# FNet block after squared-ReLU attention: three streams merged by time, channel DFT first, f32 loads of q and k

## The chip, the cores and the metric

One core of one Trainium2 chip. The metric is the device time of one launch in microseconds (us); before the change its median is 1024.95 us over three runs (1024.53 to 1026.13).

## The reference, cut to what matters

The batch B is 8, with 12 heads, 448 positions S and head size 64, so a row has D = 768 values; FFN's inner size is 3072. All inputs and the output are f32.

```python
scores = scale * np.matmul(q, k.transpose(0, 1, 3, 2))     # scale = 1/8
attn = np.maximum(scores, 0.0) ** 2 / S
x = np.matmul(attn, v)                                     # then heads side by side: (B, S, 768)
X = np.fft.fft(np.fft.fft(x, axis=1), axis=2)              # over positions, then over channels
u = x + np.real(X)
un = (u - mean) / np.sqrt(var + 1e-06)                     # over the 768 channels
out = u + np.maximum(un @ w_ch1, 0.0) @ w_ch2
```

## The kernel before, in words

All matmuls take bf16 operands. The kernel is written with a tile framework: the program gives instructions in an order, which is their priority; a scheduler with a model of the machine fixes each engine's queue from it at compile time, gives out the buffers of each tag, and sets the semaphores. On the chip every engine works through its queue in order. SP (which only starts DMAs), GpSimd (POOL) and the others have one queue each.

A batch has a front and an FFN part. The front (`front`, L361 on) is attention, then mixing. Attention (L171) takes two heads at a time (six such pairs, m). q and k come by casting DMAs on GpSimd's queue (L74), DVE copies them into another layout (L80), PE transposes them (L179, L180) into a PSUM tile, DVE copies them out as qT and kT (L187 to L189). For each of four blocks of key positions c, PE makes scores of two heads (L195), ACT applies ReLU (L198, rsc), DVE squares (L200, sq), and PE multiplies with v (L202), which adds up in av over the four blocks. DVE scales av into xT (L205). All the PSUM tiles of the front have one tag with three buffers of two banks (psA); FFN has two of one bank (psF).

Mixing (L210) transposes xT (L218), adds and subtracts positions s and S-s (xs, xa, L223, L224), takes the DFT over positions (L236), then over channels (L253) with half the outputs by symmetry, forms u for four row sets (DVE and GpSimd, L275, L276), its statistics and un (L304), and transposes un with an identity or a reversed one (L314) into unT. The rows of u go to a DRAM tile usc: the rows with natural order from u directly (112 rows, L284), the reversed ones after a shuffle on DVE into urev, in four blocks of 31 or 32, 32, 32 and 17 or 16 rows (L288, L292).

FFN works on groups of 384 or 512 rows (8 groups; a pair of batches gives one of each). The first matmul has 24 output blocks j of six matmuls each (L339), with ReLU on ACT (L342) into one hT tile per j. The second (L352) goes over 128-row chunks and two halves of 384 columns, 24 matmuls each; DVE adds the residual o (L354), which SP reloads from usc (L347), and SP stores the rows (L356). The tile o has the tag "o" with two buffers; urev has the same tag.

The program's order is front(0), front(1), then for each b: front(b+2), ffn(b). Weights are loaded once, by casting DMAs on GpSimd's queue (L92, L99), between the loads of the first two batches.

Of the kernel before, what the change touches and what calls it, by code (L numbers as in the profile page):

```python
# [9 lines left out]
FP32 = mybir.dt.float32  # L10
BF16 = mybir.dt.bfloat16
I32 = mybir.dt.int32
# [9 lines left out]

@with_exitstack
def kernel(
# [14 lines left out]
    R1 = R + 1  # L39
    MC = D // 128  # L40
    JC = FF // 128
    NQ = S + 2
    COL = [0, R1, 2 * R1, 2 * R1 + R]
    ROWS = [R1, R1, R, R]
    NS = S // 2 + 1
    KH = D // 4 + 1
    HG = 4
    NG = H // HG

# [12 lines left out]
    def psF():  # L62
        return psum.tile([128, 512], FP32, name="psF", tag="F", bufs=2)


    def load_qkv(b):
        tiles = []
        for g in range(NG):
            hs = slice(g * HG, (g + 1) * HG)
            row = []  # L70
            for nm, src in (("q", q), ("k", k), ("v", v)):
                t = work.tile([R, 2 * HG, 2 * Dh], BF16, name=f"{nm}n", tag=f"{nm}n",
                              bufs=4 if nm == "v" else 2)
                nc.gpsimd.dma_start(  # L74
                    out=t, in_=src[b, hs].rearrange("h (f p j) d -> p (h f) (j d)", f=2, j=2))
                t = t.rearrange("p (h f) (j d) -> p (f j) h d", f=2, j=2)
                if nm != "v":

                    o = work.tile([R, 4, HG, Dh], BF16, name=f"{nm}r", tag=f"{nm}r", bufs=2)
                    nc.vector.tensor_copy(o, t)  # L80
                    t = o.rearrange("p c h d -> p c (h d)")
                row.append(t)
            tiles.append(row)
        return tiles
# [19 lines left out]
    ident = const.tile([128, 128], BF16, name="ident")  # L104
    make_identity(nc, ident)
    ubot = []
    for i in range(2):
        t = const.tile([128, D], FP32, name=f"ubot{i}")
        nc.gpsimd.memset(t[96:128, :], 0.0)
        ubot.append(t)  # L110

    rev = const.tile([128, R1], BF16, name="rev")
    nc.gpsimd.memset(rev, 0.0)
    nc.gpsimd.affine_select(out=rev, in_=rev, compare_op=ALU.not_equal, fill=1.0, base=-R,
                            pattern=[[1, R1]], channel_multiplier=1)
    zero_t = const.tile([128, 1], FP32, name="zero_t")
    nc.gpsimd.memset(zero_t, 0.0)
    eps_t = const.tile([128, 1], FP32, name="eps_t")
    nc.gpsimd.memset(eps_t, 1e-6)
    qT_bufs = []  # L120
    for i in range(3):
        t = const.tile([128, R1 + 1 + 4 * R], BF16, name=f"qT{i}")
        nc.gpsimd.memset(t[:, R:R + 2], 0.0)
        qT_bufs.append(t)

    def sincos(dst, y, n, p):

        r = work.tile([128, 4 * KH], FP32, name="dftr", tag="o", bufs=2)
        nc.vector.tensor_scalar(r[:p, :n], y[:p, :n], float(2 ** 23), float(2 ** 23),
                                op0=ALU.add, op1=ALU.subtract)  # L130
        nc.vector.tensor_tensor(y[:p, :n], y[:p, :n], r[:p, :n], op=ALU.subtract)
        nc.scalar.activation(dst, y[:p, :n], AF.Sin, bias=zero_t[:p], scale=2.0 * math.pi)

    def build_dft():

        seq = const.tile([R1, 4, NS], BF16, name="seqm")
        col = work.tile([128, 2 * KH], FP32, name="dcol", tag="qs", bufs=1)
        row = const.tile([128, 8], FP32, name="drow")
        nc.gpsimd.iota(col[:, 0:NS], pattern=[[1, NS]], base=0, channel_multiplier=0,
                       allow_small_or_imprecise_dtypes=True)  # L140
        nc.gpsimd.iota(row[:, 0:2], pattern=[[1, 2]], base=0, channel_multiplier=2,
                       allow_small_or_imprecise_dtypes=True)
        nc.vector.tensor_scalar(row[:, 0:2], row[:, 0:2], 1.0 / S, None, op0=ALU.mult)
        for t in range(2):
            y = work.tile([128, 4 * KH], FP32, name="dfty", tag="u", bufs=2)
            for i in range(2):
                nc.vector.tensor_scalar(y[:R1, i * NS:(i + 1) * NS], col[:R1, 0:NS],
                                        row[:R1, i:i + 1], 0.25 if t == 0 else 0.0,
                                        op0=ALU.mult, op1=ALU.add)
            sincos(seq[:, 2 * t:2 * t + 2, :].rearrange("p a s -> p (a s)"), y, 2 * NS, R1)  # L150

        col2 = work.tile([128, 2 * KH], FP32, name="dcol2", tag=f"t{ALU.add}", bufs=1)
        nc.gpsimd.iota(col2, pattern=[[1, 2], [2, KH]], base=0, channel_multiplier=0,
                       allow_small_or_imprecise_dtypes=True)
        nc.gpsimd.iota(row[:, 4:7], pattern=[[128, 3]], base=0, channel_multiplier=1,
                       allow_small_or_imprecise_dtypes=True)
        nc.vector.tensor_scalar(row[:, 4:7], row[:, 4:7], 1.0 / D, None, op0=ALU.mult)
        chan = []
        for m in range(3):
            t = const.tile([128, 2, 2 * KH], BF16, name=f"chan{m}")  # L160
            y = work.tile([128, 4 * KH], FP32, name="dfty", tag="u", bufs=2)
            for i in range(2):
                nc.vector.tensor_scalar(y[:, i * 2 * KH:(i + 1) * 2 * KH], col2,
                                        row[:, 4 + m:5 + m], 0.25 if i == 0 else 0.0,
                                        op0=ALU.mult, op1=ALU.add)
            sincos(t.rearrange("p a s -> p (a s)"), y, 4 * KH, 128)
            chan.append(t)
        return seq, chan


    def attention(b, tiles):  # L171
        xT = []
        for m in range(MC):
            qn, kn, vn = tiles[m // (HG // 2)]
            h0 = (2 * m) % HG
            pt = psA(BF16)
            for c in range(4):
                hs = slice(h0 * Dh, (h0 + 2) * Dh)
                nc.tensor.transpose(pt[:, 0, c * R:(c + 1) * R], qn[:, c, hs], ident[:R, :R])  # L179
                nc.tensor.transpose(pt[:, 1, c * R:(c + 1) * R], kn[:, c, hs], ident[:R, :R])  # L180
            qT = qT_bufs[m % 3]
            kT = work.tile([128, S], BF16, name="kT", tag="kT", bufs=3)
            pq = pt[:, 0, 0:S].rearrange("p (c r) -> p c r", c=4)

            qa = qT[:, 0:4 * R1].rearrange("p (c r) -> p c r", c=2)[:, :, 0:R]
            qb = qT[:, R1 + 1:R1 + 1 + 4 * R].rearrange("p (c r) -> p c r", c=2)[:, :, 0:R]
            nc.vector.tensor_copy(qa, pq[:, 0:2, :])  # L187
            nc.vector.tensor_copy(qb, pq[:, 2:4, ::-1])
            nc.vector.tensor_copy(kT, pt[:, 1, 0:S])  # L189
            av = psA()  # L190
            for c in range(4):
                sc = psA()
                for e in range(2):
                    ps = slice(e * Dh, (e + 1) * Dh)
                    nc.tensor.matmul(sc[:R, e, 0:NQ], lhsT=kT[ps, c * R:(c + 1) * R], rhs=qT[ps, 0:NQ],  # L195
                                     start=True, stop=True)
                r = work.tile([R, 2, NQ], BF16, name="rsc", tag="rsc", bufs=2)
                nc.scalar.activation(r, sc[:R, :, 0:NQ], AF.Relu)  # L198
                s = work.tile([R, 2, NQ], BF16, name="sq", tag="sq", bufs=3)
                nc.vector.tensor_tensor(s, r, r, op=ALU.mult)  # L200
                for e in range(2):
                    nc.tensor.matmul(av[e * Dh:(e + 1) * Dh, 0, 0:NQ], lhsT=vn[:, c, h0 + e, :],  # L202
                                     rhs=s[:, e, :], start=(c == 0), stop=(c == 3))
            x = work.tile([128, NQ], BF16, name="xT", tag=f"xT{m}", bufs=1)
            nc.vector.tensor_scalar(x, av[:, 0, 0:NQ], 1.0 / (64.0 * S), None, op0=ALU.mult)  # L205
            xT.append(x)
        return xT


    def mix(b, xT, seq, chan, unT):  # L210
        xn, xs, xa = [], [], []
        for par in range(2):
            n = ROWS[2 * par]
            px = psA(BF16)
# [152 lines left out]
    def front(b):  # L367
        xT = attention(b, loaded.pop(b))
        if b + 2 < B:
            loaded[b + 2] = load_qkv(b + 2)  # L370
# [45 lines left out]
```

## Time and profile before

| | us |
|---|---|
| median of three runs | 1024.95 |
| lowest, highest | 1024.53, 1026.13 |
| the profiled execution | 1024.24 |
| its span, first to last instruction | 1022.4 |
| PE, DVE, ACT, GpSimd busy in the span | 766.5, 413.4, 324.8, 117.3 |
| mean granted clock of PE | 0.824 |

PE's granted clock has two levels, 1.2 GHz (0.5) and 2.4 GHz (1.0). PE's matmuls overlap in the records: the mean duration of one is longer than the distance from one start to the next, and the busy time counts overlaps once. A chain of waits is followed back from the last instruction to what released each one.

### The profile page before, as it was taken

Reading aid. Unit: us, or ns where it says so; the run is one execution under the profiler, and the core shown is the slowest. Engines: PE = TensorE matmul, PEld = TensorE weight load, DVE = VectorE, ACT = ScalarE, POOL = GpSimd, SP = SyncE. Lnnn points to the kernel's source line nnn. Section 1 sums busy time; section 2 is a strip of 40 time slices with the busy share of each in tenths; the row PEclk is TensorE's granted clock in tenths of the full one; section 3 lists DMA queues with packets and bytes.
Section 4 is the critical chain, followed back from the end, with each engine's and each line's share of the span. In section 5 each row is a group of like instructions: output and inputs, shape, how many; then the busy total and the mean of one; then the engine's idle time right before and its main releaser. Section 6 shows DMA issues by size and latency. Waiting matters only on the chain.

```text
span 1022.4 us, 11062 instructions
## 1 busy us (share of the span) xinstructions
PE 766.5 (75%) x4404; PEld 406.9 (40%) x4416; DVE 413.4 (40%) x862; ACT 324.8 (32%) x484; POOL 117.3 (11%) x139
## 2 busy tenths in 40 slices
PE   2653995566599563999499764799679865599998
PEld 1222443224254232545254323444444424366554
DVE  3477457445402546155700547235720345400001
ACT  2441761432124422065114431146104442122220
POOL 6411012011100102011200112000200000100000
PEclk9996998556599656999799756799979955699999
DMA  9993242242311332253220332332030000321202
GB/s 143 202 203 65 28 46 47 35 43 21 115 31 11 36 35 85 78 62 37 83 64 1 36 37 45 104 66 28 23 109 16 1 1 13 106 90 31 62 10 84
DMA packets 83716, 59.70 MB, mean 58 GB/s; under 512 B 68304, under 2 KB 71376, under 8 KB 83664
## 3 DMA queue, kind: packets, MB, share of 16 engines
q0 software_dynamic: 70528, 25.96, 21.4%
q1 hardware_dynamic: 13136, 33.04, 11.2%
q8 instruction: 34, 0.56, 0.2%
q14 instruction: 18, 0.15, 0.0%
HBM read 62.91 MB, written 22.02 MB: 83 GB/s over the span
## 4 chain that ended last, share of the span: by engine, by line
PE 65%; DVE 17%; ACT 9%; DMA 5%; issue 2%; POOL 0%; SPq 0%; ACTq 0%; DVEq 0%; POOLq 0%
PE psF L352 21%; PE psF L339 21%; PE psA L202 7%; ACT rsc L198 7%; PE psA L195 7%; DVE sq L200 3%; DMA usc<-urev 3%; PE psA L179 2%; PE psA L218 2%; DVE stats L280 2%; PE psA L236 2%; PE psA L253 2%; DMA o<-usc 1%; PE psA L180 1%; DVE u L276 1%
## 5 line engine op out<-in xcount | busy, mean ns | idle before, releaser
L352 PE MATMUL psF<-w,hT 128*128 128x384 bf16 x1344 | 239.5, 336 | 11.8 <-DVE o L354 11.8
L198 ACT ACTIVATE rsc<-psA 112x900 bf16<-112x900 f32 x192 | 168.9, 918 | 220.5 <-PE psA L195 220.5
L339 PE MATMUL psF<-unT,w 128*128 128x384 bf16 (+1 forms) x1140 | 237.1, 354 | 1.6 <-ACT hT L342 0.6
L200 DVE TENSOR_TENSOR sq<-rsc 112x900 bf16<-112x900 bf16 x192 | 120.3, 626 | 172.1 <-ACT rsc L198 172.1
L352 PEld LDWEIGHTS <-hT 128*128 128x128 bf16 x1344 | 133.4, 101 | 106.5 <-issue 29.7
L342 ACT ACTIVATE hT<-psF 128x384 bf16<-128x384 f32 (+1 forms) x192 | 104.0, 543 | 215.5 <-PE psF L339 214.4
L339 PEld LDWEIGHTS <-w 128*128 128x128 bf16 x1152 | 107.5, 98 | 114.6 <-issue 21.3
L202 PE MATMUL psA<-sq,vn 112*64 112x450 bf16 x384 | 93.5, 475 | 63.1 <-DVE sq L200 61.8
L354 DVE TENSOR_TENSOR o<-psF,o 128x384 f32<-128x384 f32 x56 | 30.6, 556 | 228.3 <-PE psF L352 212.4
L195 PE MATMUL psA<-qT,kT 64*112 64x450 bf16 x384 | 88.7, 494 | 37.2 <-DVE kT L189 18.0
L314 PE MATMUL psA<-ident,un 112*128 112x112 bf16 x96 | 18.7, 296 | 99.3 <-DVE un L304 99.3
L202 PEld LDWEIGHTS <-vn 112*64 112x64 bf16 x384 | 29.2, 118 | 118.4 <-issue 83.6
L195 PEld LDWEIGHTS <-kT 64*112 64x112 bf16 x384 | 32.6, 154 | 87.7 <-issue 54.3
L314 PEld LDWEIGHTS <-un 112*128 112x128 bf16 (+1 forms) x192 | 16.2, 137 | 109.3 <-DVE un L304 109.3
L187 DVE COPY qT<-psA 128x224 bf16<-128x224 bf16 x48 | 13.1, 273 | 114.1 <-PE psA L180 114.1
L74 POOL DMA_DIRECT2D qn<-in_q_dram x24 | 20.0, 835 | 315.8 <-DVE qr L80 239.5
L276 POOL TENSOR_TENSOR ubot<-tpm,xn 113x383 f32<-113x383 f32 (+1 forms) x16 | 13.5, 846 | 264.7 <-DVE tpm L262 237.3
L239 ACT ACTIVATE ytmp<-psA 128x450 f32<-128x450 f32 x24 | 13.1, 546 | 81.8 <-PE psA L236 60.8
L179 PE MATMUL psA<-ident,qr 112*128 112x112 bf16 x192 | 32.5, 254 | 8.4 <-DVE qr L80 8.0
L74 POOL DMA_DIRECT2D vn<-in_v_dram x24 | 19.7, 819 | 163.2 <-PE psA L202 161.4
L205 DVE TENSOR_SCALAR xT<-psA 128x450 bf16<-128x450 f32 x48 | 30.1, 627 | 16.0 <-PE psA L202 14.3
L180 PE MATMUL psA<-ident,kr 112*128 112x112 bf16 x192 | 32.8, 256 | 2.3 <-DVE kr L80 2.3
(68 smaller groups left out, 598.7 us busy)
## 6 DMA issues: line engine op xcount, KB each, us to landing
o<-usc SPq DMA_DIRECT2D x28, 384.0 KB
qn<-in_q_dram POOLq DMA_DIRECT2D x24, 224.0 KB, 4.2
kn<-in_k_dram POOLq DMA_DIRECT2D x24, 224.0 KB, 4.9
vn<-in_v_dram POOLq DMA_DIRECT2D x24, 224.0 KB, 4.1
usc<-u SPq DMA_DIRECT2D x16, 336.0 KB
w<-in_moe_w_ch_dram POOLq DMA_DIRECT2D x12, 384.0 KB, 11.9
w<-in_moe_w_ch_dram POOLq DMA_DIRECT2D x4, 1152.0 KB, 22.8
usc<-urev SPq DMA_DIRECT2D x40, 96.0 KB
```

The source lines that it names most:

```text
L74: nc.gpsimd.dma_start(out=t, in_=src[b, hs].rearrange("h (f p j) d -> p (h f) (j d)", f=2, j=2))
L179: nc.tensor.transpose(pt[:, 0, c * R:(c + 1) * R], qn[:, c, hs], ident[:R, :R])
L180: nc.tensor.transpose(pt[:, 1, c * R:(c + 1) * R], kn[:, c, hs], ident[:R, :R])
L195: nc.tensor.matmul(sc[:R, e, 0:NQ], lhsT=kT[ps, c * R:(c + 1) * R], rhs=qT[ps, 0:NQ], start=True, stop=True)
L198: nc.scalar.activation(r, sc[:R, :, 0:NQ], AF.Relu)
L200: nc.vector.tensor_tensor(s, r, r, op=ALU.mult)
L202: nc.tensor.matmul(av[e * Dh:(e + 1) * Dh, 0, 0:NQ], lhsT=vn[:, c, h0 + e, :], rhs=s[:, e, :], start=(c == 0), stop=(c == 3))
L314: nc.tensor.matmul(pu[:, e, i * R:(i + 1) * R], lhsT=uns[i][:n, ms], rhs=idn, start=True, stop=True)
L339: nc.tensor.matmul(ph[:, 0:N], lhsT=w1_sb[m][j // (JC // 2)][:, jj * 128:(jj + 1) * 128], rhs=unT[:, m, 0:N], start=(m == 0), stop=(m == M ...
L342: nc.scalar.activation(h[:, 0:N], ph[:, 0:N], AF.Relu)
L352: nc.tensor.matmul(pc[:, 0:D // 2], lhsT=hT[j][:, c * 128:(c + 1) * 128], rhs=w2_sb[j // 6][:, j % 6, hs], start=(j == 0), stop=(j == JC - 1))
L354: nc.vector.tensor_tensor(o[:, hs], pc[:, 0:D // 2], o[:, hs], op=ALU.add)
```

## The change

The order of the program becomes a merge of three kinds of streams by a clock of their own: each stream says, at each yield, how much time its last piece stands for, and the piece of the stream with the least time comes next. Attention of all batches is one stream, each batch's mixing one, FFN of all batches one. FFN of batch b is let in when mixing b has been written out. The scheduler is told to use its timeline model.

Inside attention, scores run two steps ahead of the products with v (LAG). q and k are loaded as f32 by SP, two groups of four heads ahead, and the re-layout copy casts them; v stays on GpSimd's queue, with three buffers. kT is copied by ACT. The order of positions in qT is natural and mirrored halves (225 columns each), so that sums and differences of s and S-s are taken on xT itself (fold), and of channels c and c+384 (A and Bm). Mixing takes the DFT over channels first, straight from these, 225 positions in two chunks of 113 and 112, then over positions with 385 output columns. There is no shuffle: the mirrored rows go to a second DRAM tile ubo as they are, and a DMA from DRAM to DRAM copies them reversed into usc. The reload of o is asked for in the middle of the first matmul, and o shares its buffers with no tile of mixing; the output needs one store per chunk. The PSUM tiles are psS (two of two banks), psT and psF (two of one bank each).

The diff, cut to its core:

```diff
-    def psA(dtype=FP32):
-        return psum.tile([128, 2, n], dtype, name="psA", tag="A", bufs=3)
+    def psS():
+        return psum.tile([128, 2, 512], FP32, name="psS", tag="S", bufs=2)
+    def psT(dtype=FP32):
+        return psum.tile([128, n], dtype, name="psT", tag="T", bufs=2)
...
+                if nm == "v":
+                    t = work.tile([R, 2 * HG, 2 * Dh], BF16, name="vn", tag="vn", bufs=3)
+                    nc.gpsimd.dma_start(out=t, in_=src)
+                else:
+                    t = work.tile([R, 2 * HG, 2 * Dh], FP32, name=f"{nm}n", tag=f"{nm}n", bufs=QB)
+                    nc.sync.dma_start(out=t, in_=src)
...
+    def heads(b, m):
+        if h0 == 0:
+            relay(g)
+            load_group("qk")
+        pt = psF(BF16) if b == 0 else psT(BF16)
...
+        nc.scalar.activation(kT, pt[:, S:2 * S], AF.Copy)
...
+        for i in range(4 * MC + LAG):
+            if i < 4 * MC:
+                if c == 1 and m + 1 < MC:
+                    hd[m + 1] = heads(b, m + 1)
+                if c == 3 and m % 2 == 0:
+                    load_group("v")
+                sc = scores(i)
...
+                    x = work.tile([128, NQ], BF16, name="xT", tag=f"xT{m}", bufs=1)
+                    nc.vector.tensor_scalar(x, av[:, 0:NQ], 1.0 / (64.0 * S), None, op0=ALU.mult)
+                    nc.vector.tensor_tensor(f[:, 0, :], x[:, 0:NS], x[:, NS:NQ], op=ALU.add)
+                    nc.vector.tensor_tensor(f[:, 1, :], x[:, 0:NS], x[:, NS:NQ], op=ALU.subtract)
...
+        for n0, n1 in SC:
+            pp = psS()
+            for t in range(2):
+                for kp, Y, kw in ((0, A, KH), (1, Bm, KH - 1)):
+                    for m in range(3):
+                        nc.tensor.matmul(pp[:n, t, kp * KH:kp * KH + kw], lhsT=Y[m][:, t, n0:n1],
+                                         rhs=chan[m][:, t, kp * KH:kp * KH + kw],
+                                         start=(m == 0), stop=(m == 2))
...
+            nc.sync.dma_start(out=usc[r0 + s0:r0 + s1, :], in_=us[0][:n])
+            lo, hi = (1, R1) if ch == 0 else (0, n - 1)
+            t0 = r0 + S - s0 - (hi - 1)
+            nc.sync.dma_start(out=ubo[t0:t0 + hi - lo, :], in_=us[1][lo:hi])
+            nc.sync.dma_start(
+                out=usc[t0:t0 + hi - lo, :].rearrange("t (a d) -> a t d", a=2)[:, ::-1, :],
+                in_=ubo[t0:t0 + hi - lo, :].rearrange("t (a d) -> a t d", a=2))
...
+        for j in range(JC):
+            if j in (JC // 2, JC // 2 + 2):
+                reload()
...
+                if m % 3 == 2:
+                    yield 3 * N / 2400
...
+    constants()
+    load_group("qk")
+    load_group("v")
+    load_group("qk")
+    load_group("v")
+    seq, chan = build_dft()
     load_w1(0)
     load_w1(1)
     load_w2()
...
+            n = 4 * MC + LAG + 1
+            rate = STEP0 if b == 0 else STEP1 if b == 1 else (73.0 / n)
+            for d in attention(b, *x):
+                yield d * rate
+            spawn(mix_stream(b, x))
...
+            while b not in mixed:
+                yield 1.0
+            for d in ffn(*groups[b]):
+                yield d * (STRETCH if b < B - 1 else 1.0)
...
+    STEP0, STEP1, STRETCH = 1.1, 2.4, 1.33
+    spawn(attention_stream())
+    while streams:
+        s = min(streams)
+        clock[0] = s[0]
+        d = next(s[2], None)
...
+    with tile.TileContext(tc.nc, schedule_with_timeline_sim=True) as t:
+        body(t, *args)
```

## Rows read from the trace of the kernel before

**Rows 1.** The page: busy us of each engine; two of its costliest groups.

```profile
PE 766.5 (75%) x4404; PEld 406.9 (40%) x4416; DVE 413.4 (40%) x862; ACT 324.8 (32%) x484; POOL 117.3 (11%) x139
...
L198 ACT ACTIVATE rsc<-psA 112x900 bf16<-112x900 f32 x192 | 168.9, 918 | 220.5 <-PE psA L195 220.5
...
L200 DVE TENSOR_TENSOR sq<-rsc 112x900 bf16<-112x900 bf16 x192 | 120.3, 626 | 172.1 <-ACT rsc L198 172.1
```

**Rows 2.** Busy time by stretch: us, length, engines' busy us, PEclk, DMA share, GB/s.

```profile
0.00:104.00 104.00, 47.22 (x246) 24.66 (x247) 57.99 (x124) 33.48 (x43) 35.03 (x60) 0.91 1.00 151
104.00:158.00 54.00, 52.80 (x344) 25.36 (x342) 28.38 (x59) 32.91 (x52) 7.36 (x9) 0.99 0.40 39
158.00:271.00 113.00, 57.02 (x327) 32.04 (x325) 65.33 (x139) 32.27 (x44) 18.95 (x17) 0.58 0.30 48
...
409.00:483.00 74.00, 73.37 (x463) 37.50 (x462) 30.15 (x61) 31.15 (x47) 7.36 (x9) 0.98 0.40 61
483.00:510.00 27.00, 13.43 (x106) 9.19 (x104) 18.69 (x41) 5.43 (x10) 5.79 (x4) 0.78 0.24 69
```

**Rows 3.** SP's longest wait from 104 to 271 us: total us, times, longest.

```profile
SPq L284 <- DVE u L276: 146.7, 4, 74.8
```

**Rows 4.** Timeline of SP's issues in the same stretch: start us, us, what.

```profile
264.77 1.71 SPq L292 DMA_DIRECT2D usc<-urev  x4
267.36 2.14 SPq L347 DMA_DIRECT2D o<-usc  x2
```

**Rows 5.** The chain of waits at the end: start us, us, what, pieces merged.

```profile
955.46 10.74 PE psF L339 x49
...
986.27 31.21 PE psF L352 x192
```

**Rows 6.** Timeline of PE near 119 us, clock 1.0: start us, us, what.

```profile
118.71 0.40 PE L195 MATMUL psA<-qT,kT 64*112 64x450 bf16 x2
119.04 0.34 PE L339 MATMUL psF<-unT,w 128*128 128x384 bf16 x1
119.38 0.38 PE L202 MATMUL psA<-sq,vn 112*64 112x450 bf16 x2
119.69 0.22 PE L179 MATMUL psA<-ident,qr 112*128 112x112 bf16 x1
...
120.09 0.33 PE L339 MATMUL psF<-unT,w 128*128 128x384 bf16 x1
```

**Rows 7.** The chain of waits from 483 to 512 us.

```profile
489.83 1.27 PE psA L253 x13
...
498.80 8.11 DMA usc<-urev
```

**Rows 8.** The page: GB/s in 40 slices of 25.6 us; issues of the weight loads.

```profile
GB/s 143 202 203 65 28 46 47 35 43 21 115 31 11 36 35 85 78 62 37 83 64 1 36 37 45 104 66 28 23 109 16 1 1 13 106 90 31 62 10 84
...
w<-in_moe_w_ch_dram POOLq DMA_DIRECT2D x12, 384.0 KB, 11.9
w<-in_moe_w_ch_dram POOLq DMA_DIRECT2D x4, 1152.0 KB, 22.8
```

**Rows 9.** Groups of PE's matmuls from 420 to 480 us: count | busy us, mean ns | idle before.

```profile
L339 PE MATMUL psF<-unT,w 128*128 128x384 bf16 x144 | 29.6, 328 | 0.1
L352 PE MATMUL psF<-w,hT 128*128 128x384 bf16 x93 | 15.4, 326 | 0.0
L202 PE MATMUL psA<-sq,vn 112*64 112x450 bf16 x46 | 8.8, 374 | 0.0
L195 PE MATMUL psA<-qT,kT 64*112 64x450 bf16 x43 | 7.5, 377 | 0.3
L179 PE MATMUL psA<-ident,qr 112*128 112x112 bf16 x20 | 2.6, 214 | 0.1
```

**Rows 10.** Busy time, clock, DMA share and GB/s around the stores of u.

```profile
255.50:257.50 2.00, 0.00 (x0) 0.00 (x0) 2.00 (x7) 0.00 (x0) 0.00 (x0) 0.53 0.55 167
261.20:262.40 1.20, 0.62 (x5) 0.23 (x3) 1.20 (x4) 0.00 (x0) 1.20 (x1) 0.50 0.11 20
```

More of the change, by code (lines that the diff above doesn't have):

```diff
@@ L23, with body @@
 @with_exitstack
-def kernel(
+def body(
     ctx: ExitStack,
@@ L56 @@
     usc = dram.tile([B * S, D], FP32, name="usc")
-    def psA(dtype=FP32):
+    ubo = dram.tile([B * S, D], FP32, name="ubo")
+    def psS():
+        return psum.tile([128, 2, 512], FP32, name="psS", tag="S", bufs=2)
+    def psT(dtype=FP32):
         n = 512 if dtype == FP32 else 1024
-        return psum.tile([128, 2, n], dtype, name="psA", tag="A", bufs=3)
[L62 to L84, printed above, removed]
@@ new lines, in body, with load_group @@
+    loads = [[None] * 3 for _ in range(B * NG)]
+    loaded = {"qk": 0, "v": 0}
+    def load_group(what):
+        i = loaded[what]
+        if i == B * NG:
+            return
+        loaded[what] += 1
+        b, g = divmod(i, NG)
+        hs = slice(g * HG, (g + 1) * HG)
+        for nm, src in (("q", q), ("k", k), ("v", v)):
+            if nm in what:
+                src = src[b, hs].rearrange("h (f p j) d -> p (h f) (j d)", f=2, j=2)
+                if nm == "v":
[4 more added lines that the diff above has]
+                    nc.sync.dma_start(out=t, in_=src)
+                loads[i]["qkv".index(nm)] = t
@@ L101, in load_w2 @@
             w2_sb[i] = t
[L104 to L168, printed above, removed]
@@ L171, in attention @@
[L171 to L196, printed above, removed]
@@ new lines, in attention, with scores @@
+    def attention(b, xT, A, Bm):
+        def scores(i):
+            m, c = divmod(i, 4)
+            qT, kT = hd[m][0:2]
+            sc = psS()
+            for e in range(2):
+                ps = slice(e * Dh, (e + 1) * Dh)
+                nc.tensor.matmul(sc[:R, e, 0:NQ], lhsT=kT[ps, c * R:(c + 1) * R], rhs=qT[ps, :],
+                                 start=True, stop=True)
+            return sc
+        hd = {0: heads(b, 0)}
+        yield 1.0
+        F, sc, sqs = [], {}, {}
+        for i in range(4 * MC + LAG):
+            if i < 4 * MC:
+                m, c = divmod(i, 4)
+                if c == 1 and m + 1 < MC:
[3 more added lines that the diff above has]
+                sc = scores(i)
@@ L204, in attention @@
[L204 to L214, printed above, removed]
+                sq = work.tile([R, 2, NQ], BF16, name="sq", tag="sq", bufs=3)
+                nc.vector.tensor_tensor(sq, r, r, op=ALU.mult)
@@ new lines, in mix @@
+                x = work.tile([R1, D], BF16, name="xn", tag=f"xn{i}", bufs=1)
+                nc.scalar.activation(x[:n], px[:n, 0:D], AF.Copy)
+                xs.append(x)
+                yield 0.7
+            pq = psS()
+            for t in range(2):
+                for i, (n0, n1) in enumerate(SC):
+                    nc.tensor.matmul(pq[:n, t, 0:KN], lhsT=seq[:n1 - n0, t, i, s0:s1],
+                                     rhs=pcs[i][:n1 - n0, t, 0:KN], start=(i == 0), stop=(i == 1))
+            qs = work.tile([R1, KN], FP32, name="qs", tag="qs", bufs=1)
@@ new lines, in mix @@
+            yield 2.5
+        if b % 2 == 0:
+            g0 = work.tile([128, MC, 512], BF16, name="unT", tag="unT", bufs=2)
+            tail = work.tile([128, MC, S - 384], BF16, name="tail", tag="tail", bufs=1)
+            groups.append((b * S, 384, g0))
+            tails.append(tail)
+            unT = [(g0, 0, 0, 384), (tail, 0, 384, S)]
+        else:
+            g1 = work.tile([128, MC, 512], BF16, name="unT", tag="unT", bufs=2)
+            groups.append(((b - 1) * S + 384, 512, g1))
+            nc.gpsimd.tensor_copy(g1[:, :, 0:S - 384], tails.pop())
+            unT = [(g1, S - 384, 0, S)]
```

303 lines of the change are left out of this document (182 added, 121 removed).

## The prediction

> **What bounds the kernel now.** I read the page first, then busy time by stretch, the waits and order of SP's queue, and the chain of waits. The page [rows 1] has TensorE (PE) busy for three quarters of the span and no other engine above 40%, so it names PE, but as a mean over two kinds of stage. The stretches [rows 2] part them. From 104 to 158 us and from 409 to 483 PE is busy for 98 and 99% of the time at a granted clock of 0.99 and 0.98 (2.4 GHz nearly throughout): attention runs there with FFN matmuls between its steps. From 158 to 271 PE is busy for 57 of 113 us at 0.58, so mostly at 1.2 GHz: attention and mixing run alone. From 483 to 510 mixing alone keeps PE busy for 13 of 27 us. The first 104 us have no FFN work by construction.
>
> Why is there no FFN work from 158 to 271, when group 0 was ready? SP's queue tells [rows 3, 4]: the reload of the residual (o<-usc, L347) is issued at 267.4, behind the four-piece stores of batch 2's u, and in that stretch SP waited 146.7 us for DVE to make u. The tile o shares its two buffers with the reversed copy urev of a later batch, so the reload stands behind work that comes much later. FFN's second matmul needs o to free its PSUM tile, its first needs hT, and the whole stream stands. So the bound is a starved PE, not PE's work.
>
> **PE's work, priced at 2.4 GHz.** An FFN matmul of 384 columns takes 31.21/192 = 0.1625 us, one of 512 columns 10.74/49 = 0.219 [rows 5]. There are 1344 + 576 of the first and 576 of the second: 312.0 + 126.2 = 438.2. By start-to-start times [rows 6] a pair of scores takes 119.04 - 118.71 = 0.33, a pair of AV products 0.31, and eight transposes 0.40; 192 of each pair and 48 sets of eight give 122.9 + 19.2. None of this changes.
>
> Mixing changes. Channel first, it has 192 matmuls of 193 columns at 1.27/13 = 0.098 [rows 7] = 18.8, 64 of 385 columns at 0.1625 = 10.4 (96 + 96 of 225 columns go), 192 transposes of 128 columns at 0.057 (0.05 scaled by 128/112) = 11, and 192 of 112 at 0.05 = 9.6: about 50. In all 630 us, 78.8 per batch, of which 24 per batch are attention and mixing.
>
> **Parts that stay beside PE.** DVE: copies of k, xn, the sums xs and xa, yp, ym and the shuffle go: 160 instructions of the size of a square's 0.626 us [rows 1], about 100 us. Folds and differences (144 of 225 or 450 elements, by the square's 900 elements 0.16 to 0.31 us each), half the DFT copy (16) and a re-layout that now reads f32 (48, each up to 0.5 us longer) come: between 40 and 90, I take 70. DVE goes from 413 [rows 1] to about 385 us. ACT gains 48 copies of k, 32 of xn and 16 of the channel result, 0.4 to 0.8 us each by the 0.918 for 900 elements [rows 1], and loses 24 ytmp: from 325 to about 370. Beside 640 us of PE, both are some 60% used: no bound, but denser than the 41 and 42% of the stretch 409 to 483 [rows 2]. Without that cover each of their microseconds would count, as it does in the opening. GpSimd loses 48 DMA issues; SP gains them. SP's q/k loads are asked for two head groups ahead, about 48 us, and can hide a wait of that length.
>
> **The opening, 97 us.** Before, FFN begins at about 104 [rows 2]. The first steps get shorter: scores run two steps ahead, so a step costs max(ACT 0.918 [rows 1], DVE 0.626 plus an estimated 0.75 for its share of copies and folds) = 1.4 us, 24 steps 34 us. But the third v load is emitted inside attention, behind all weight loads on GpSimd's one queue. Weights are 12 x 384 + 4 x 1152 KB = 9.44 MB; at 203 GB/s [rows 8] that is 46.5 us. Add two v loads (2.3), six f32 q/k loads of 0.46 MB on the same saturated engines (7 to 14, by 406 GB/s read or 203 written; I take 9), a start of 3 and a landing of 2 (both estimates): v arrives at 63, while its first use is due at 14 (an estimate: first loads, and the DFT tables on DVE) + 16 x 1.4 = 36. PE has nothing else then: three squared tiles and two score tiles fill up and attention stands. After 63 come the eight AV steps, five at full pace (9 us), then mixing alone, 27 us now [rows 2], 25 taken: FFN starts at 97.
>
> **The steady part, 653 us.** What is left is 630 - 24, less 6 of batch 1's attention done beside mixing: 600. The last group's 62 us are pure FFN at the prices above. The other 538 run interleaved. How well does that go? From 420 to 480 [rows 9]: 237 FFN matmuls x 0.1625 = 38.5, 23 pairs x 0.31, 21.5 x 0.33 and 40 transposes x 0.05 are 54.7 of 60 us, 0.91. It holds a step of attention per 2.8 us, the 73/27 = 2.7 of the new merge. So 538/0.91 = 591, + 62 = 653.
>
> **Hand-overs, 10.** FFN of batch b is emitted just as mixing b ends. Mixing's chain is 27 us now with nothing beside it, and the merge gives it 22 units. At about 3 us each for seven batches, half of it filled by attention: 10.
>
> **The residual by way of DRAM: 0 to 60, 5 taken.** The shuffle and four row blocks become a store of 113 or 112 rows to usc, one of 112 or 111 rows to ubo, and a copy from ubo to usc that SP issues only when ubo has landed; behind it in SP's queue stand q/k loads, reloads and output stores. No row shows a copy from DRAM to DRAM or a store of 113 rows. The nearest: the 112-row store moves its 0.34 MB in the two microseconds at 167 GB/s; in 261.2 to 262.4, the tail of the 31- and 17-row stores, a busy share of 0.11, under two of 16 engines, moves 20 GB/s [rows 10], and those 48 rows, 147 KB, hold the chain for 8.11 us [rows 7], 18 GB/s. So 113 rows cost 2 to 347 KB/20 = 17.4 us, a copy 2 to 17. The ends are far apart; of the row counts shown, 112 and 32 are fast and 31 and 17 slow, and 113 and 111 are odd like the slow ones, so I take 17 for both stores and 10 for a copy. In line on one engine the four transfers of a batch land 17 + 10 + 17 + 10 = 54 us after the first starts, some 12 before mixing ends: 42 after its end. The reload is first used some 40 us after mixing ends (24 blocks j and a half chunk, beside attention), and the chunk that needs copied rows 10 later: covered, narrowly; hence 5. As a load, the four take 38 to 68 us of that engine per batch, its sixteenth of some 7.6 MB of other traffic (q, k, v, reload, output) at 20 GB/s another 24: 62 to 92, against 78.8/0.91 = 87 of PE.
>
> The Trainium skill (DMA: Bandwidth & Descriptors, section "Why a DMA increments its semaphore by 16 and not by 1") says that a transfer is spread over the largest number up to 16 that divides the outermost extent of both sides. The 31- and 17-row rows agree; by it 113 rows go to one engine, 111 to three, and the copy, whose outermost extent is its two halves, to two: 17 + 6 + 2 x 9 to 17 = 41 to 57 us in place of 38 to 68, and the 5 stay. If transfers spread over all engines whatever their rows, the term is 0 and the sum 5 lower.
>
> **End and sum.** After the last matmul the reload's add and store took 1022.4 - (986.27 + 31.21) = 4.9. Span: 97 + 653 + 10 + 5 + 5 = 770. The profiled execution takes 1024.24 with a span of 1022.4, so 1.8 lie around it, and it stands 0.7 below the median of the runs, 1024.95. Forecast: 772.
>
> **Rivals.** *v is not late* (the scheduler or the rings let it pass): FFN starts at 14 + 34 + 25 = 73, total 748; with interleaving at 0.97 instead of 0.91 and no hand-over loss 702. For: 0.97 is still under the 73.4 of 74 us that PE is busy in [rows 2]. Against: one queue, and earlier loads come first in the program. Chance 0.18.
>
> *SP's wait shows*: the landing of ubo is late behind the 113-row store, and reloads, stores and q/k loads stand behind it in order, as they stand behind u now [rows 3, 4]. If 5 to 13 us of each batch come through: 810 to 870. For: the margin of 8 us above. Chance 0.17.
>
> *The merge holds only half*: each engine's order is fixed from a model; where the chip is later, PE waits in order. A pair of batches now takes 239 us (271 to 510), 119 each; the new one 87; halfway is 103: 97 + 7 x 103 + 62 = 880. If nothing held, the change would not do what it says, and the time would lie between 97 + 7 x 119 + 62 = 992 and today's. For: denser ACT and DVE. Against: the fed stretches come from such an order too. Chance 0.09, of it 0.01 for no change.
>
> *Slower*: one DMA engine becomes the bound. It must need over 87 + (1025 - 772)/7 = 123 us per batch, so each copy over (123 - 58)/2 = 32 us, twice the 17 of a slow store of as many bytes. At 35 us a copy the total is 772 + 7 x (128 - 87) = 1059. For: no row shows DRAM to DRAM. Against: no row shows so low a rate. Chance 0.04.
>
> **How the numbers follow.** The forecast keeps 0.52, with its own range 730 to 810 (interleaving 0.87 to 0.96, opening 90 to 105). To hold eight in ten, the range takes in the early v and most of SP's wait: 700 to 870. What can be told from no change is 0.2%, 2 us (the runs of before span 1.6). Faster 0.94, same 0.01, slower 0.05.
>
> **What would show it.** FFN's first matmul near 97 and attention standing before it, its AV waiting for vn: the opening. PE's busy share above 0.95 with clock near 1.0 from there to the end: the merge. A store of 113 rows in flight for over 15 us: one engine; PE or DVE waiting for o<-usc: SP's wait shows. A clock at 0.5 in stretches after 110 us, or PE often waiting for DVE's squares, would make the prediction wrong; so would an opening under 80.

## The result and the profile after

The changed kernel takes 796.8 us (median of four runs, 796.57 to 797.37) against 1024.7 before: a ratio of 0.7775 [0.7762, 0.7789]. The forecast was 772, the range 700 to 870. The profiled execution takes 796.57 with a span of 794.8, so again 1.8 us lie around it.

The page of the changed kernel, engines and the two groups of [rows 1]:

```profile
PE 689.3 (87%) x4288; PEld 360.9 (45%) x4288; DVE 388.3 (49%) x894; ACT 359.1 (45%) x555; POOL 68.6 (9%) x96
...
L233 ACT ACTIVATE rsc<-psS 112x900 bf16<-112x900 f32 x192 | 172.6, 920 | 143.2 <-PE psS L217 103.3
...
L235 DVE TENSOR_TENSOR sq<-rsc 112x900 bf16<-112x900 bf16 x192 | 118.5, 620 | 85.8 <-ACT rsc L233 83.4
```

PE is busy for 87% of the span instead of 75, DVE and ACT stand at about half. Busy time by stretch, with the columns of [rows 2]:

```profile
0.00:104.00 104.00, 42.10 (x225) 21.54 (x226) 51.03 (x119) 38.26 (x49) 19.95 (x44) 0.99 0.93 175
104.00:158.00 54.00, 48.58 (x313) 24.71 (x312) 36.20 (x92) 35.69 (x61) 4.68 (x6) 0.83 0.48 109
158.00:271.00 113.00, 107.72 (x662) 55.70 (x660) 53.99 (x119) 50.83 (x77) 8.69 (x9) 0.95 0.32 82
271.00:300.00 29.00, 22.62 (x160) 12.58 (x159) 16.70 (x42) 8.60 (x14) 2.03 (x2) 0.94 0.25 82
...
270.00:276.00 6.00, 6.00 (x41) 3.24 (x39) 5.93 (x15) 3.76 (x6) 0.42 (x1) 1.00 0.06 16
276.00:282.00 6.00, 6.00 (x43) 3.29 (x42) 6.00 (x13) 1.95 (x3) 2.03 (x2) 1.00 0.41 141
282.00:288.00 6.00, 6.00 (x38) 2.94 (x36) 4.19 (x14) 1.76 (x3) 0.00 (x0) 1.00 0.06 26
```

Where PE was busy for 57 of 113 us at a clock of 0.58 it now is for 107.7 at 0.95: this starved stretch is filled. Two things are not as forecast. The first 104 us are no fuller than before, and there is a hole from 271 to 300.

**The opening.** The chain of waits of its first 120 us:

```profile
10.98 29.70 DMA qn<-in_q_dram
40.68 30.13 DMA kn<-in_k_dram
...
119.32 1.39 PE psF L389 x4
```

FFN's first matmul comes at 119.3, not at 97, and what the chain runs through is not v but loads of q and k of some 30 us each. The re-layouts in DVE's timeline (in brackets how long DVE stood before one, and for what):

```profile
27.46 0.69 DVE L181 CAST qkr<-qn 112x1024 bf16<-112x1024 f32 x1 [11.50 <-DMA qn<-in_q_dram]
39.96 0.69 DVE L181 CAST qkr<-kn 112x1024 bf16<-112x1024 f32 x1 [11.14 <-DMA kn<-in_k_dram]
48.53 0.69 DVE L181 CAST qkr<-qn 112x1024 bf16<-112x1024 f32 x1 [3.74 <-DMA qn<-in_q_dram]
...
70.91 0.69 DVE L181 CAST qkr<-kn 112x1024 bf16<-112x1024 f32 x1 [4.69 <-DMA kn<-in_k_dram]
```

These are q and k of group 2, the last of batch 0, then q of group 3 and, three re-layouts on, k of group 4, both batch 1's (a batch has three groups). Each stands in DVE's queue ahead of squares of batch 0 and holds them. There are two buffers for k, so the load of group 4's k could be asked for, at 40.68, only when group 2's late k had been re-laid out (39.96 + 0.69). The line of q in the chain stops where this request starts: that load itself lands only at 48.4, when its re-layout begins. By 71 us PE has done 16 AV matmuls, eight steps of batch 0's 24. v of group 2, asked for at 33.2 and 39.0 us on its way, lands at 72 as well. The DMA queues between 11 and 40 us (q0 is GpSimd's, with the weights, q1 SP's, with q and k; packets, MB, share) say why q and k are late:

```profile
q0 software_dynamic: 2405, 5.10, 91.2%
q1 hardware_dynamic: 2396, 1.20, 19.9%
```

The two queues get the same number of packets, 2405 and 2396 (and 3603 and 3611 from 40 to 70 us). A packet of the weights holds 2.1 KB on average, one of f32 q or k 0.5 KB, so SP's queue moves 1.20 MB where GpSimd's moves 5.10. The Trainium skill (DMA: Bandwidth & Descriptors, section "Queues, rings and completion order") says that a DMA engine goes round between the queues that have work for it, a packet at a time; the two counts agree, if its packets are those that the trace counts.

**The hole.** SP's issues around it (start us, us, what):

```profile
270.86 0.25 SPq L335 DMA_DIRECT2D usc<-u  x1
271.16 4.93 SPq L339 DMA_DIRECT2D ubo<-u  x1
276.18 1.27 SPq L409 DMA_DIRECT2D out_dram<-o  x1
287.56 0.59 SPq L340 DMA_DIRECT2D usc<-ubo  x1
288.49 0.68 SPq L380 DMA_DIRECT2D o<-usc  x1
```

The first is the store of 113 rows. From 270 to 276 and again from 282 to 288 the DMA engines' busy share is 0.06, one of 16, at 16 to 26 GB/s: 347 KB take some 16 us, near the 17 priced. Between them, from 276 to 282, the share is 0.41 at 141 GB/s: there the other engines do their part of what was issued behind. But everything issued behind has a share on that one engine too, and ends only when it is free: of the 16 landings that the trace has for the output store, 15 lie before 280.2, the last at 288.5. The chain there (start us, us, what):

```profile
276.18 12.29 DMA out_dram<-o
288.49 9.81 DMA o<-usc
```

and the waits of the whole execution (total us, times, longest):

```profile
DVE o L408 <- DMA o<-usc: 34.8, 3, 11.7
...
DVE qkr L181 <- DMA qn<-in_q_dram: 23.8, 5, 11.5
DVE qkr L181 <- DMA kn<-in_k_dram: 23.2, 5, 11.1
...
PE psF L389 <- DVE o L408: 18.9, 3, 6.4
```

The output store takes 12 us, the reload has to wait for it, and DVE and then PE stand for o, three times in the span (from 276, 452 and 628 us on). The two rows between are the opening's: DVE stood 47 us for q and k.

### The profile page after: what moved, and what is told of

Its sections match the earlier page's. It is cut to its first block, busy times and chain, and to the rows that moved or that the text cites. A ratio compares the mean times of both kernels' runs of the same rounds, so it can differ in the third digit from the quotient of the medians.

```text
span 794.8 us, 10782 instructions
## 1 busy us (share of the span) xinstructions
PE 689.3 (87%) x4288; PEld 360.9 (45%) x4288; DVE 388.3 (49%) x894; ACT 359.1 (45%) x555; POOL 68.6 (9%) x96
## 4 chain that ended last, share of the span: by engine, by line
PE 65%; DMA 17%; DVE 11%; issue 3%; ACT 2%; POOL 1%; POOLq 0%; SPq 0%; DVEq 0%; ACTq 0%
PE psF L389 30%; PE psF L404 17%; PE psS L217 6%; PE psT L244 5%; DMA kn<-in_k_dram 5%; DMA out_dram<-o 5%; DMA qn<-in_q_dram 4%; DMA o<-usc 4%; PE psS L273 2%; DVE sq L235 2%; DVE stats L320 2%; DVE un L331 1%; PE psS L365 1%; PE psT L291 1%; DVE u L314 1%
## 5 line engine op out<-in xcount | busy, mean ns | idle before, releaser
L389 PE MATMUL psF<-unT,w 128*128 128x512 bf16 (+1 forms) x1152 | 257.4, 365 | 19.1 <-DVE o L408 18.9
L233 ACT ACTIVATE rsc<-psS 112x900 bf16<-112x900 f32 x192 | 172.6, 920 | 143.2 <-PE psS L217 103.3
L244 PE MATMUL psT<-sq,vn 112*64 112x450 bf16 x384 | 78.7, 408 | 49.9 <-DVE sq L235 48.9
L217 PE MATMUL psS<-qT,kT 64*112 64x450 bf16 x384 | 79.9, 427 | 12.6 <-ACT kT L207 8.7
L248 DVE TENSOR_SCALAR xT<-psT 128x450 bf16<-128x450 f32 x48 | 29.9, 623 | 29.1 <-PE psT L244 29.0
L368 ACT ACTIVATE unT<-psS 128x768 bf16<-128x768 f32 (+1 forms) x24 | 20.3, 864 | 51.6 <-PE psS L365 51.6
L181 DVE CAST qkr<-qn 112x1024 bf16<-112x1024 f32 x24 | 16.6, 691 | 37.4 <-DMA qn<-in_q_dram 23.8
L320 DVE BATCH_NORM_STATS2 stats<-u 113x6 f32<-113x384 f32 (+1 forms) x64 | 32.3, 544 | 0.9 <-POOL u L314 0.5
L302 ACT ACTIVATE qs<-psS 113x385 f32<-113x385 f32 (+1 forms) x16 | 7.9, 492 | 48.9 <-PE psS L299 48.8
L207 ACT ACTIVATE kT<-psT 128x448 bf16<-128x448 bf16 x42 | 22.9, 544 | 12.6 <-DVE qT L206 12.6
L293 ACT ACTIVATE xn<-psT 113x768 bf16<-113x768 bf16 (+1 forms) x32 | 25.6, 806 | 5.8 <-DVE u L314 4.7
L181 DVE CAST qkr<-kn 112x1024 bf16<-112x1024 f32 x24 | 16.7, 696 | 23.2 <-DMA kn<-in_k_dram 23.2
```

The lines of the kernel that those rows point to most:

```text
L244: nc.tensor.matmul(av[e * Dh:(e + 1) * Dh, 0:NQ], lhsT=vn[:, c, h0 + e, :], rhs=sq[:, e, :], start=(c == 0), stop=(c == 3))
L248: nc.vector.tensor_scalar(x, av[:, 0:NQ], 1.0 / (64.0 * S), None, op0=ALU.mult)
L293: nc.scalar.activation(x[:n], px[:n, 0:D], AF.Copy)
L320: nc.vector.bn_stats(stats[:n, hf, :], u[:n, hf * (D // 2):(hf + 1) * (D // 2)])
L389: nc.tensor.matmul(ph[:, 0:N], lhsT=w1_sb[m][j // (JC // 2)][:, jj * 128:(jj + 1) * 128], rhs=unT[:, m, 0:N], start=(m == 0), stop=(m == M ...
```

## The experiments

Times are medians; a ratio is to runs of the kernel before on the same chip. Diffs are to the changed kernel, where not said otherwise.

**e1_v_first: v of group 2 asked for ahead of the weights.**

```diff
     load_group("v")
+    load_group("v")
     seq, chan = build_dft()
```

> The third v load is asked for ahead of the weights, all else as after the change (796.8 us). If the late v holds the opening, as the prediction says, its 24 us of waiting go: FFN's first matmul comes near 95 in place of 119, the total near 773. If the q/k loads hold it (re-layouts of group 2 at 65.5 and 70.9 us, each load about 10 us beside the weights), v lands early, the re-layouts stay near 71, and the total stays within 3 us of 797.

792.3 us, 0.7737 [0.7719, 0.7754]; FFN from 116.8. The chain still runs through q (from 11.0 for 21.1 us) and k (from 32.1 for 37.4, to 69.5), and by 71 us nine AV steps are done instead of eight. So v in time gains 4.5 us by itself, a little more than the second theory allowed: q and k in DVE's queue hold attention anyway. The expectation is wrong on one point: the re-layouts at 65.5 and 70.9 us are those of group 4, not of group 2.

**e2_gate: the weights held back until k of group 2 has landed.** A one-column copy from kn into each weight tile makes its load wait.

```diff
+            nc.gpsimd.tensor_copy(t[0:R, 0:1], gate[:, 0, 0:1])
             nc.gpsimd.dma_start(
...
+            nc.gpsimd.tensor_copy(t[0:R, 0, 0:1], gate[:, 0, 0:1])
             nc.gpsimd.dma_start(
...
+                    load_group("v")
+                    gate = loads[2][1]
+                    load_w1(0, gate)
+                    load_w1(1, gate)
+                    load_w2(gate)
```

> The weight loads wait for k of group 2 (one element of each weight tile is written from it first), so batch 0's q, k and v have the DMA engines to themselves; v of group 2 is also asked for ahead of the weights. If the loads beside the weights hold the opening, batch 0's loads are in by 15 us, attention ends near 50, FFN starts at 78 to 88 in place of 119, and the total falls by 30 to 40 us, to 757 to 767. If the opening goes at the pace of the engines, FFN starts past 105 and the total is above 783; if the delayed weights hold FFN, its first matmul waits for w, near 100.

784.7 us, 0.7662 [0.765, 0.7675]; FFN only from 110.0. Its waits of PE from 20 to 110 us:

```profile
PE psT L246 <- DVE sq L237: 19.4, 10, 10.3
PE psT L246 <- DMA vn<-in_v_dram: 16.4, 1, 16.4
```

q and k came early, but v of the next batch, asked for behind all 16 weight loads on GpSimd's queue, took 37 us to land, and PE stood 16.4 us for it with batch 0's mixing behind it in its order.

**e7_gate_v: the second FFN weights called later in the program.**

```diff
+                if b == 0 and x_steps == 18:
+                    load_w2(loads[2][1])
```

> As e2_gate, but the four loads of w2 are asked for after two more v loads, and w2 is not tied to k. In e2_gate PE stood 16.4 us before an AV product of batch 1 whose v lay behind all weights, and mixing 0 stood behind it in PE's queue. If that is what was left of the opening's wait, FFN starts at 85 to 93 in place of 110 and the total is 758 to 768. If another load takes its place (q/k of batch 1, w2), FFN starts past 100 and the total is above 775.

785.6 us, 0.7669 [0.7658, 0.7681]: a miss. The place in the program is only a priority. The scheduler issued these four loads at 6.55 us, ahead of the gated ones, so the bytes in the opening stayed the same. The chain of waits:

```profile
32.55 35.84 DMA kn<-in_k_dram
...
68.42 0.69 DVE qkr L182
...
110.32 1.44 PE psF L390 x4
```

The load that lands at 68.4 is k of group 4 again. DVE stood 10.3 us for it, and PE as long for the squares behind it.

**g5_gate_each: the second weights wait, by data, for v of group 4.**

```diff
+            nc.gpsimd.tensor_copy(t[0:R, 0, 0:1], gate[:, 0, 0:1])
...
+                if b == 0 and x_steps == 18:
+                    load_w2(loads[4][2])
```

> The changed kernel with the third v load ahead of the weights, the first FFN weights (12 loads) held back until k of group 2 has landed and the second FFN weights (4 loads) until v of group 4 has landed. The last attempt held back only the first weights: the second ones were still issued at 6.55 us, so the opening still carried all the weights' bytes ahead of batch 1's k (landed 68.4, after 35.8 us). Theory (the opening is held by which bytes come first, at some 215 GB/s in all): q, k and v of batches 0 and 1 land before 55, attention of batch 0 does not stop, the FFN's first matmul comes at 85 to 97 instead of 110, time 758 to 775. Rival (batch 0's mixing is in order behind batch 1's attention on VectorE and that sets the FFN's start whatever the loads do): FFN from 105 on, time 780 to 787. If the second weights now come too late, PE waits for w after its first FFN group instead.

786.5 us, 0.7681 [0.7654, 0.7708]. FFN begins at 95.5, inside the bounds, but the time is that of the rival. The chain of waits shows where the gain went:

```profile
78.21 31.58 DMA ubo<-u
...
110.54 14.52 DMA ubo<-u
...
125.08 9.27 DMA usc<-ubo
...
135.23 6.30 DMA kn<-in_k_dram
```

Batch 0's 113-row store now meets the second weights: 32 us in place of 17. SP's queue waits for it, and q and k of batch 2's last group are asked for at 134.8 only; PE is busy for 27.7 of the 38 us from 120 to 158. Neither theory had that.

**e3_spread: stores and copy spread over all engines** (113 rows as 112 + 1, 111 as 96 + 15, the copy in 16 parts).

```diff
-            nc.sync.dma_start(out=usc[r0 + s0:r0 + s1, :], in_=us[0][:n])
+            for e0, e1 in ((0, R), (R, n)):
+                if e1 > e0:
+                    nc.sync.dma_start(out=usc[r0 + s0 + e0:r0 + s0 + e1, :], in_=us[0][e0:e1])
...
+            for e0, e1 in ((0, 96), (96, L)) if L % 16 else ((0, L),):
...
-                out=usc[t0:t0 + hi - lo, :].rearrange("t (a d) -> a t d", a=2)[:, ::-1, :],
+                out=usc[t0:t0 + hi - lo, :].rearrange("t (a d) -> a t d", a=16)[:, ::-1, :],
```

> The 113-row store is cut in 112 and 1, the 111-row store in 96 and 15, and the copy from ubo to usc has 16 parts outermost in place of 2 (192-byte pieces). If one DMA engine's work (0.06 of the engines at 26 GB/s from 282 to 288 us) holds SP and so the reload, PE's waits for DVE's add (18.9 us in three places) go, and what follows them at low clock: total 767 to 780. If the wait is SP's order alone (landing, then copy, then reload, whatever the spread), the waits stay above 12 us and the total above 787.

771.2 us, 0.7527 [0.7514, 0.754]: 25.6 us less, as expected.

**e3_stores: the stores alone** (the copy stays in two parts).

> Of e3_spread only the stores (113 rows as 112 and 1, 111 as 96 and 15); the copy from ubo to usc keeps its two parts. If the 17 us of the 113-row store, which hold up ubo's landing and then the copy, are the wait, most of the 26 us of e3_spread come from here: 771 to 780. If the copy on few engines is, little changes: 788 to 797.

770.6 us, 0.7524 [0.7509, 0.7539]: all of it is the stores, and the copy costs nothing that can be told. Its busy time by stretch:

```profile
270.00:276.00 6.00, 6.00 (x41) 3.11 (x39) 5.93 (x16) 3.49 (x6) 0.64 (x1) 1.00 0.57 185
...
265.00:300.00 35.00, 35.00 (x247) 19.16 (x245) 26.40 (x60) 17.64 (x29) 5.42 (x6) 1.00 0.36 107
440.00:480.00 40.00, 40.00 (x283) 20.72 (x282) 28.21 (x67) 24.10 (x41) 4.19 (x5) 1.00 0.52 144
```

The same six microseconds have a DMA share of 0.57 and 185 GB/s instead of 0.06 and 16, and PE works from 265 to 300 us without a pause.

**g6_gate_each_split: the opening of g5 with the stores split.**

> The same opening together with the 113-row and 111-row residual stores split (112 + 1 and 96 + 15 rows). The two losses lie in different stretches (before 120 us, and at the FFN's odd group ends from 276 on), so by the theory the gains add: the run above less 24 to 28 us, 732 to 750. Rival (an earlier FFN runs into the mixing of the next batch, which then ends last): 750 to 771, with waits for mixing at the hand-overs in place of the opening.

742.9 us, 0.7244 [0.7219, 0.7268], the fastest of all runs; FFN from 89.4. The gains add, and more than add: the split takes 43.6 us off g5, against 26.2 off the changed kernel. The collision with the second weights is gone: PE is busy for all of the 38 us from 120 to 158, for 27.7 in g5. The bounds were hit in part by chance, since they were worked out from the time that g5 was expected to take and did not.

**e4_before_own_urev: the kernel before, with a tag of its own for urev** (v gives up one buffer for it).

```diff
-                               bufs=4 if nm == "v" else 2)
+                               bufs=3 if nm == "v" else 2)
...
-                    w = work.tile([128, D], FP32, name="urev", tag="o", bufs=2)
+                    w = work.tile([128, D], FP32, name="urev", tag="urev", bufs=1)
```

> The kernel before, with a buffer of its own for the reversed copy urev (one, and three v buffers in place of four, to make room), so that o shares with nothing of mixing. If the place of the reload behind a later batch's u starves FFN, FFN fills the stretches from 158 to 271 and from 328 to 409: the total falls from 1025 to between 850 and 950. If the order of the program (front of b+2 ahead of FFN of b) starves it, whatever buffer o has, the total stays above 990.

805.8 us, 0.7871 [0.7856, 0.7886]: 218 of the 228 us, by one tag, and faster than the bounds expected. Its starved stretch, beside [rows 2]:

```profile
158.00:271.00 113.00, 100.92 (x660) 52.09 (x667) 72.05 (x151) 43.63 (x66) 19.80 (x18) 0.98 0.37 68
```

PE is busy for 100.9 us there at a clock of 0.98, with the old program order and no merge.

**g4_before_urev_split: that, with the 31- and 17-row stores as 16 + 15 and 16 + 1.**

> The kernel before with two fixes alone: a tag of its own for urev (805.8 us by itself), and its reversed stores of 31 and 17 rows split into 16 + 15 and 16 + 1, so that none runs on one DMA engine. Some 8 us of store stand in its chain of waits in each of 8 batches. Theory (these stores end the wait of the FFN there as the 113-row store did in the changed kernel): 760 to 785, the old order would then be about as fast as the change without its own fix. Rival (the stores lie beside mixing's other work, the chain only passes through them): 800 to 808.

793.8 us, 0.7747 [0.7734, 0.7759]: 12 us less, between the two. The odd stores cost the old kernel too, but partly beside other work.

**e8_no_merge: the changed kernel in the program order of before.**

```diff
-    while streams:
-        s = min(streams)
...
+    front(0)
+    front(1)
+    for b in range(B):
+        if b + 2 < B:
+            front(b + 2)
+        for d in ffn(*groups[b]):
+            pass
```

> All of the change but the merge: the program's order is again front(0), front(1), then front(b+2) and FFN of b; the tiles, loads, DFT order and the model are those after the change. If o's place among the buffers was all that starved PE, the scheduler fills the gaps by itself and the total stays within 25 us of 797. If the merge is what feeds PE, as the prediction has it, starved stretches come back and the total is above 850.

840.8 us, 0.8209 [0.8195, 0.8223], between the two theories. So the merge looked worth 44 us. But the chain of waits names something else:

```profile
268.34 22.60 DMA ubo<-u
...
369.50 16.89 DMA o<-usc
...
464.69 21.90 DMA ubo<-u
```

and again a late o at 564.7 and a late ubo at 660.9.

**g3_no_merge_split: the same order with the stores split.**

> The changed kernel with the program order of before (840.8 us by itself: the merge looked worth 44 us) and the residual stores split as in the run of 771 us. Question: what is the merge worth once no store runs on one DMA engine? Theory (the unmerged order lost its time to the same stores, which stand three times with some 22 us in its chain, and twice more as a late o of 17 us): 775 to 800, the merge is then worth 5 to 30 us. Rival (the merge itself keeps PE fed, the stores cost both orders the same 26 us): 808 to 820.

751.4 us, 0.7343 [0.7331, 0.7355], below both theories. Without the one-engine stores the merge does not help: it costs 20 us (771.2 to 751.4, both with the copy in 16 parts). In the merged order (the run with the stores alone split), busy time by stretch shows dips near the ends of a batch's mixing:

```profile
180.00:200.00 20.00, 14.57 (x108) 8.37 (x107) 17.80 (x43) 8.18 (x13) 2.50 (x3) 0.92 0.53 176
...
360.00:380.00 20.00, 17.00 (x112) 8.04 (x112) 12.12 (x33) 13.42 (x20) 2.11 (x3) 0.91 0.39 102
...
680.00:700.00 20.00, 14.66 (x95) 9.27 (x95) 13.76 (x31) 5.62 (x9) 4.59 (x4) 0.87 0.42 141
```

and in the old order only the first of them is left:

```profile
180.00:200.00 20.00, 16.33 (x115) 8.43 (x115) 12.89 (x36) 7.80 (x13) 2.00 (x2) 0.91 0.76 198
...
360.00:380.00 20.00, 19.80 (x117) 8.07 (x117) 10.74 (x25) 15.32 (x23) 0.84 (x1) 1.00 0.46 116
...
680.00:700.00 20.00, 18.94 (x104) 9.19 (x105) 0.56 (x1) 9.85 (x16) 0.00 (x0) 1.00 0.28 75
```

From 120 to 700 us PE is idle for 18.4 us in the merged order and 7.6 in the old one. That is only part of the 20 us: by the pages of the two runs with the copy in 16 parts, PE's busy time is 680.6 us in the merged order and 666.4 in the old one, so 14 us are longer work, with a granted clock of 0.971 against 0.986 (0.87 to 0.92 in the dips), and 7 us are idle time over the whole span. In the old order the front of batch b+2 stands ahead of FFN b, so each mixing is done before its FFN is wanted; the merge lets FFN in just as mixing ends, and the chain of mixing shows. That is an account of the difference; no run moves the lead alone, and only one setting of the merge's rates was tried.

**e5_default_model: no timeline model in the scheduler.**

```diff
-    with tile.TileContext(tc.nc, schedule_with_timeline_sim=True) as t:
+    with tile.TileContext(tc.nc) as t:
```

> All of the change but the timeline model: the scheduler's default model makes the queues of the same merged program. If the merged order itself carries the gain, the total stays within 15 us of 797. If the model's order of the queues matters, PE waits more often for DVE's squares and ACT and the total is above 820.

902.6 us, 0.8818 [0.8799, 0.8837]: on the merged order the model is worth 106 us. PE's waits there (total us, times, longest):

```profile
PE psS L365 <- DVE un L331: 41.5, 15, 8.4
PE psT L244 <- DVE sq L235: 21.7, 22, 8.9
```

Mixing's transposes stand in PE's queue too early and wait for un 41.5 us; in the changed kernel that wait is 8.2. The total is on the side of the second theory, but its sign is not there: PE waits less for squares than in the changed kernel, 21.7 us against 48.9. The wait that grew most is the one for un, by 33 us; PE's busy time is longer too, 730.0 us against 689.3 at a clock of 0.893 against 0.957.

**Where the 228 us come from**, as one path of runs (227 by the runs of before beside them):

| kernel | us | step |
|---|---|---|
| before | 1024.0 | |
| urev with its own tag | 805.8 | -218 |
| and its stores split | 793.8 | -12 |
| the new front, loads and timeline model, in the old order, stores split | 751.4 | -42 |
| and the merge | 771.2 | +20 |
| and the stores unsplit: the changed kernel | 796.8 | +26 |

In the step of 42 us PE's busy time falls from 703.9 to 666.4 by the two pages, 37.5 us (the second trace lacks 21 of 4288 matmuls, which may be up to 5 of them). The shorter mixing is not most of it. Counted from each matmul's start to the next one's, mixing's fall from 67.9 to 55.3 us, but FFN's second matmul from 246.2 to 219.2, though these are the same 1344. The two pages' rows for it, before and after the step:

```profile
L354 PE MATMUL psF<-w,hT 128*128 128x384 bf16 x1344 | 257.5, 330 | 3.3 <-DVE o L356 2.5
...
L408 PE MATMUL psF<-w,hT 128*128 128x384 bf16 x1344 | 230.2, 326 | 0.0
```

In the first, 166 of them stand right before a matmul of attention, and these take 258 (AV) or 291 ns (scores) to the next start, in place of 163 (medians); in the second, 3 do. By this count, how finely the queue alternates between the two kinds costs PE time although PE does not stand. No run changes that alone, and which part of the step brings it (the front, the loads or the model) is not known. The steps depend on their order: with unsplit stores the merge gains.

## Why the prediction was right, and where it was not

**The bound: right.** A PE starved by o behind urev, not PE's work: one tag gave 218 us. What the prediction did not see is that this one cause holds nearly the whole net gain: what the rest gained, 54 us, the merge and the stores nearly gave back, 46. Its forecast was built up from the new schedule and had no term for the old schedule without the shared tag, so it could not say that the merge would add next to nothing.

**Work beside PE: right.** DVE 388.3 us for 385, ACT 359.1 for 370; neither became a bound in the steady part. A squared tile took 620 ns, a ReLU 920.

**The opening, 97 us: wrong, 119.3.** The step that failed is the price of the loads. The prediction added "six f32 q/k loads of 0.46 MB on the same saturated engines", 9 us, to the time of the weights, and let 16 attention steps run before v came. It shared bytes where the engines share packets, so attention stood for q and k from 16 us on, and it did not ask what DVE's order does when batch 1's loads are late too: their re-layouts stand among batch 0's squares. At 71 us eight AV steps were done, not 16. Late v was real, 72 for the 63 forecast, but not the bound alone (e1). So 8 of the 22 us are the later landing (70.9 for 63). The other 14 are what came after it, 48.4 us for 9 + 25, with 16 AV steps to go instead of eight: eight more at the forecast's own 1.4 us are 11. With the bytes in order, 26 AV steps were done by 71 us, k of group 4 landed at 42.6, and FFN began at 89.4 (g6).

**The steady part and the hand-overs, 653 + 10: too high.** With the stores split, FFN's first matmul is at 118.7 and the last ends at 763.1: 644.4 us against 663. Interleaving was nearer 0.95 than 0.91, a share read off the old order: less the last group (63.6 us from 699.5) and 16.6 us of PE idle in the dips at 180, 360, 520 and 680, 564 us are left for the 538 (the low clock after the dips still in it). The hand-overs cost those 16.6, not 10.

**The residual by way of DRAM, 5: wrong, 26.** Prices of single transfers held: some 16 us, for 17, for 113 rows on one engine at 16 to 26 GB/s, and the copy took 9.3 for 10 (in g5). By the Trainium skill (DMA: Bandwidth & Descriptors, section "Why a DMA increments its semaphore by 16 and not by 1") 113 rows go to one engine and 112 to all. The shares agree: 0.06 is one of 16, and with 112 + 1 rows it is 0.57. The step that failed is "covered, narrowly". It let four transfers run in line by themselves, and took the engine's other traffic only as load. But output stores and reloads have a share on that engine as well, and stand behind the 16 us there. The loss comes three times, where an output store and a reload fall into it. Its kind was the rival *SP's wait shows*; per batch it is 26.2/7 = 3.7 us, under that rival's 5 to 13.

**End: right.** 3.9 us after the last matmul for 5. That the sum came near is in part luck, because an error stood against two: the opening +22 and the stores +21, against -19 in the steady part and its hand-overs.

**Rivals.** The merge did not hold only half, and the copy never became the bound: spread or not, 771.2 and 770.6.

**Left open.** The old order with split stores (751.4) and the ordered opening (742.9, with the merge) were not tried together. Whether mixing's lead over FFN is what the merge loses was not tried by itself, nor were other rates of the merge. The front, the loads and the timeline model were not tried apart in the old order.

## What to carry to other kernels

Before crediting a new schedule, free the one buffer that the old one waits for: a tag shared by a producer far ahead and a consumer now can put the whole queue behind the far one, and its cost is measured by one renamed tag. Price a slow transfer not by its own cover alone but by everything issued behind it that needs the same engine, and split a store whose row count leaves it on one engine. Of loads that start together on two queues, those with small packets came last here. What is needed first must be asked for first, held in order by data, since a place in the program is only a priority.

## What was not expected of the hardware

- Two DMA queues share the engines by packets, not by bytes: 2405 against 2396 packets, 5.10 against 1.20 MB in 29 us, in the opening.
- One transfer on one engine delays all that follow on its queue: a store of 112 rows and an output store issued within 6 us of it ended 16 and 12 us after their issue, though the engines' busy share was 0.06 in the six microseconds before 276 and after 282.
- SP's own issue gets long when transfers pile up: one DMA of q or k took 0.3 us to issue when the engines were free, up to 13.3 beside the weights (from 21.4 to 34.7 us); the store of 112 rows behind the 113-row one took 4.93, and 0.33 behind the split one.
- A single-engine store beside the weight loads held the store behind it for 31.6 us instead of 16.4 (g5, and the changed kernel at 271.2).
- An FFN matmul of 384 columns took 163 ns to the next matmul's start, but 258 or 291 when that one was attention's (medians of the old order with both fixes).
